# Seven block products for eight in three pairs of row tiles, inside the attention slots of an attention and mixer kernel

## The chip, the cores and the metric

One core of one Trainium2 chip. The metric is the device time of one execution in microseconds (us). The kernel is a single program of about ten thousand instructions on five engines: TensorE (PE) for matrix products, VectorE (DVE), ScalarE (ACT) and GpSimd (POOL) for elementwise work, SyncE (SP) as the queue that issues most transfers.

## The reference

Cosine attention over 8 batches of 12 heads, 448 rows, head width 64; then a mixer of a token layer and a channel layer.

```
q_n = q / (norm(q) + 1e-6);  k_n = k / (norm(k) + 1e-6)
attn = softmax(q_n @ k_n^T / tau)            # tau = 0.1
x = (attn @ v) as (8, 448, 768)
h = relu(x^T @ w_tok1) @ w_tok2              # 448 -> 256 -> 448, over the rows
u = x + h^T
out = u + relu(u @ w_ch1) @ w_ch2            # 768 -> 1536 -> 768, over the channels
```

Inputs and output are float32; the kernel multiplies in float16 and accumulates in float32.

## The kernel before

**Slots.** The work runs over 48 pairs of heads, `i` = 0 to 47, six to a batch. What is done for one `i` of the main loop is called a slot here. A slot begins with the scores of pair `i` (`score`, three tiles of 128 keys for both heads, Exp on ACT, which also leaves the softmax unnormalised), goes on with attention times values of pair `i - 1` (`pv_rest`, `pv`; DVE takes the reciprocal and scales: `x`), and then has, in the order in which PE meets them: a unit of channel work, the rest score (`score_rest`, the last 64 keys), the second token product of pair `i - 2` (`tok2`, into `u16`, transposed by a transfer on SP's queue into `ut`: `udma`), more channel units, and the first token product of pair `i - 1` (`tok1`).

**Preparing q and k.** Beside it a slot prepares later pairs. `square` and `sums` form the squared lengths of pair `i + 3` (squares on POOL or ACT, the sum on DVE), `norms` makes 1/norm for pair `i + 2` (Ln and Exp on ACT, a sum and a reciprocal on DVE), `scaled` multiplies k and q by it on POOL into a float16 tile `kq`, and `tpose_dma` transposes that by a transfer on SP's queue into `qk`, which the scores of slot `i + 2` read. SP also issues the loads of q, k and v for pairs `i + 6` and `i + 4` and the stores of the output. Every engine takes its own instructions in order.

**Buffers.** q and k tiles have 7 buffers each, v 4, `kq` 4, `qk` 4, tiles of squares 3. PSUM has two pools: `ps2` with three double banks (scores, and channel units that are called `wide`), `ps` with two single banks.

**The channel layers.** Batches 0 to 5 go through them inside the slots; the rows of a batch form three tiles of 128 and a shared tile `m = 3` that holds the last 64 rows of two batches. `m_ch1` makes one of 12 blocks of the hidden layer (six matmuls of 448 columns, Relu on ACT into `gt`). `m_ch2` makes one half (384 columns) of one row tile: 12 matmuls, then DVE adds `u` and SP stores the finished rows. Before, a queue of units with a rate for each stretch of slots (`refill`, `due`, `RATES`) decides which unit goes into which slot.

**The end.** Batches 6 and 7, and three row tiles of batch 5, go through a block form of the channel layers after the last slot. There a product of 2 x 2 blocks is made from seven block products instead of eight (`p1` to `p7`, `q1` to `q7`). It needs sums of the weight blocks: `fast_weights2` forms four sums of quarters of the second weight matrix on POOL, each in three parts; before, five parts stand in slots 40 to 44 and seven after the last slot.

Of the kernel before, what the change touches and what calls it, by code (L numbers as in the profile page):

```python
# [22 lines left out]
def kernel(  # L23
# [12 lines left out]
    nc = tc.nc  # L36
# [44 lines left out]

    cst = ctx.enter_context(tc.tile_pool(name="cst", bufs=1))
# [4 lines left out]
    att = late.enter_context(tc.tile_pool(name="att", bufs=4))  # L87
    qkv = ctx.enter_context(tc.tile_pool(name="qkv", bufs=7, side="right"))
# [14 lines left out]
    def load_first(a, src):  # L103
        t = qkv.tile([SC, QS, E], FP32, name=f"{a}f_0", tag=f"{a}f", bufs=7)
        for g, eng in ((0, nc.sync), (1, nc.scalar)):
            eng.dma_start(out=t[:, NCH * g:NCH * (g + 1)].rearrange("p c e -> p (c e)"),
                          in_=src[0, g].rearrange("(p c) e -> p (c e)", c=NCH))
        return t

    def pool_of(nm):  # L110
        return att if nm == "v" else qkv

    def load_rows(i, nm, src, bufs):
        h0 = 2 * (i % NPAIR)
        if old(i):
            t = pool_of(nm).tile([SC, QS, E], FP32, name=f"{nm}f_{i}", tag=f"{nm}f", bufs=bufs)
            nc.sync.dma_start(
                out=t[:].rearrange("p (g c) e -> p g (c e)", g=2),
                in_=src[h0:h0 + 2].rearrange("g (p c) e -> p g (c e)", c=NCH))
            return t  # L120
        t = pool_of(nm).tile([128, 2 * KC, E], FP32, name=f"{nm}f_{i}", tag=f"{nm}f", bufs=bufs)
        nc.sync.dma_start(out=t[:].rearrange("p (g c) e -> p g (c e)", g=2),
                          in_=src[h0:h0 + 2, 0:128 * KC].rearrange("g (p c) e -> p g (c e)", c=KC))
        return t

    def load_rest(i, nm, src):
        h0 = 2 * (i % NPAIR)
        t = (att if nm == "v" else rest).tile([128, HP, E], FP32, name=f"{nm}r_{i}", tag=f"{nm}r", bufs=4)
        for g in range(2):
            nc.sync.dma_start(out=t[64 * g:64 * g + 64],  # L130
                              in_=src[h0 + g:h0 + 2 * HP:2, 128 * KC:S].rearrange("j p e -> p j e"))
        return t

    def load_qk(i):
        b, h0 = i // NPAIR, 2 * (i % NPAIR)
        n = i // HP
        half.setdefault(n, {})
        st = pipe[i] = {}
        st["q"] = qkv.tile([SC, QS, E], FP32, name=f"qf_{i}", tag="qf")
        nc.sync.dma_start(out=st["q"][:].rearrange("p (g c) e -> p g (c e)", g=2),  # L140
                          in_=q[b, h0:h0 + 2].rearrange("g (p c) e -> p g (c e)", c=NCH))
        st["k"] = load_rows(i, "k", k[b], 7)
        if not old(i) and "kr" not in half[n]:
            half[n]["kr"] = load_rest(i, "k", k[b])

    def load_v(i):
        pipe[i]["v"] = load_rows(i, "v", v[i // NPAIR], 4)
        if not old(i) and "vr" not in half[i // HP]:
            half[i // HP]["vr"] = load_rest(i, "v", v[i // NPAIR])
# [15 lines left out]
    NV = 3  # L165
# [46 lines left out]
    kqs = [rest.tile([128, 2, NCH, 2, E], FP16, name=f"kq{i}", bufs=1) for i in range(4)]  # L212
    sqs = [rest.tile([128, 2 * QS, E], FP32, name=f"sq{i}", bufs=1) for i in range(3)]
# [23 lines left out]
    def square(i, a, act=False):  # L237
        st = pipe[i]
        sl, np_ = lay(i)
        if "sq" not in st:  # L240
            st["sq"] = sqs[i % 3]
        parts = [(st["kq"[a]][:], st["sq"][0:np_[a], sl[a]])]
        if a == 0 and not old(i):
            parts = [(st["k"][:], st["sq"][:, 0:2 * KC]),
                     (half[i // HP]["kr"][:, i % HP], st["sq"][:, 2 * KC])]
        for src, dst in parts:
            if act:
                nc.scalar.activation(out=dst, in_=src, func=AF.Square)  # L248
            else:
                nc.gpsimd.tensor_mul(out=dst, in0=src, in1=src)  # L250
# [33 lines left out]
    def scale_part(i, a, c0, c1, eng):  # L284
        st = pipe[i]
        if "kq16" not in st:
            st["kq16"] = kqs[i % 4]
# [5 lines left out]
    def scale(i, a, eng=None):  # L293
# [3 lines left out]
        if "kq16" not in st:  # L297
            st["kq16"] = kqs[i % 4]
# [165 lines left out]
    def m_ch1(b, ct, wide):  # L464
        if b // 2 not in gts:
            gts[b // 2] = mix.tile([128, CT, 2 * S], FP16, name=f"gt_{b // 2}", tag="gt", bufs=1)
        gt = gts[b // 2]
# [7 lines left out]

    ost = {}


    def m_ch2(b, m, lo, hi, st, wide):
        gt = gts[b // 2]  # L480
# [36 lines left out]
    def ch1_units(b):  # L517
        return [(ns(S, DT), lambda wide, ct=ct: m_ch1(b, ct, wide), False, b % 2 == 0) for ct in range(CT)]

    def ch2_units(b):  # L520
        cuts = ((0, DH, None), (DH, D, 0))
        if b == 0:
            order = [(m, c) for c in cuts for m in range(3)]
        else:
            order = [(m, c) for m in range(3) for c in cuts]
            if b == KEPT_B:
                order = [(3, c) for c in cuts]
            elif b % 2:
                order[3:3] = [(3, cuts[0])]
                order[5:5] = [(3, cuts[1])]  # L530
        return [(ns(hi - lo, CT), lambda wide, m=m, lo=lo, hi=hi, st=st: m_ch2(b, m, lo, hi, st, wide), m == 3, False)
                for m, (lo, hi, st) in order]

    HD, HC = DT // 2, CT // 2
# [67 lines left out]
    def gpart(i, b, d):  # L602
        lo = 64 * b
        return (gts["new"] if b else gts[KEPT_B // 2])[:, HC * i + 2 * d:HC * i + 2 * d + 2, lo:lo + S]

    def g_shared(i):
        nc.sync.dma_start(out=gts["new"][:, HC * i:HC * (i + 1), 0:64],
                          in_=gts[KEPT_B // 2][:, HC * i:HC * (i + 1), 384:S])
# [39 lines left out]
    def fast_weights2(n, parts=range(3)):  # L648
        def w(i, j):
            return [wc2t[:, HC * i + 2 * m:HC * i + 2 * m + 2, DH * j:DH * (j + 1)] for m in range(3)]  # L650

        t = fw.setdefault("t2", {})
        if n not in t:
            at = [(n - 1 + m) % 2 for m in range(3)]
            t[n] = [qkv.tile([128, 2, DH], FP16, name=f"t{n}w2_{m}", tag=("qf", "kf")[z]) for m, z in enumerate(at)]
        a, b = {1: (w(0, 1), w(0, 0)), 2: (w(1, 1), t.get(1)), 3: (w(1, 1), w(0, 1)), 4: (w(1, 0), t.get(2))}[n]
        for m in parts:
            tt(nc.gpsimd, t[n][m][:], a[m], b[m] if n % 2 else b[m][:], ALU.subtract)

    def fast_w2(n, j):  # L660
# [3 lines left out]
        return fw["t2"][{4: 4, 5: 1, 6: 2, 7: 3}[n]][j // 2][:, j % 2]  # L664
# [4 lines left out]
    def gtile(t, i):  # L669
        g, at = (gts["new"], t - 3) if 3 <= t < 7 else (gts[KEPT_B // 2], t if t < 3 else t - 3)  # L670
        return g[:, HC * i:HC * (i + 1), 128 * at:128 * at + 128]

    def s_tile(g, k):
        if g == 0 and k < 3:
            return qkv.tile([128, HC, 128], FP16, name=f"s{k}g_0", tag=("qf", "kf")[k - 1])[:]
# [112 lines left out]
    queue = []  # L788
    fed = [0.0, 0.0]

    def unit(wide=False, late=False):
        if queue:
            swap = late and queue[0][2] and len(queue) > 1 and not queue[1][2] and not queue[1][3]
            t, fn = queue.pop(1 if swap else 0)[:2]
            fn(wide)
            fed[0] -= t

    def due():
        return queue and fed[0] > queue[0][0] / 2

    KEPT = 6000.0
    RATES = {2 * NPAIR + 2: 4550.0, 4 * NPAIR + 2: 4100.0, 5 * NPAIR + 2: 3850.0, 6 * NPAIR + 2: 3200.0}
    LATE = NP_ALL - 10
    ACT_SQ = range(LATE - 2, NP_ALL - 3)

    def refill(b):
        new = ch1_units(b) + ch2_units(b)
        if b == 0:
            fed[1] = (sum(u[0] for u in new) - KEPT) / (NPAIR + 1)
        if b == KEPT_B:  # L810
            queue[:0] = new[:CT]
            queue[-4:-4], new = new[CT:], []
        queue.extend(new)

    with tc.manual_schedule():
# [127 lines left out]
        def side(i):  # L943
# [6 lines left out]
            elif i + 3 < NP_ALL:  # L950
                squares(i + 3)
            if i in (8, 11):
# [13 lines left out]
        for i in range(NPAIR + 1, NP_ALL):  # L966
# [18 lines left out]
            if i == NPAIR + 1:  # L985
                refill(0)
            elif pj == (3 if b - 1 == KEPT_B else 2) and 1 < b < B - 1:
                refill(b - 1)
# [4 lines left out]
            fed[1] = RATES.get(i, fed[1])  # L993
            if i == NP_ALL - HP:
                fed[1] = (sum(u[0] for u in queue) - fed[0]) / HP
            fed[0] += fed[1]
            unit(True)
# [4 lines left out]
            if i in ACT_SQ:  # L1002
                square(i + 3, 1, act=True)
            if i > NPAIR + 1:
# [3 lines left out]
            if due():  # L1008
                unit(True, True)
            while due():  # L1010
                unit()
            tok1(i - 1)
            if i + 3 < NP_ALL:
                sums(i + 3)
            if NP_ALL - 8 <= i < NP_ALL - 5:
                fast_weights2(1, (i - NP_ALL + 8,))
            if NP_ALL - 5 <= i < NP_ALL - 3:
                fast_weights2(2, (i - NP_ALL + 5,))
# [10 lines left out]
        while queue:  # L1029
            unit(True)  # L1030
# [31 lines left out]
        fast_weights2(2, (2,))  # L1062
        fast_weights2(3)
# [9 lines left out]
        fast_weights2(4)  # L1073
# [101 lines left out]
```

## Time and profile before

| | |
|---|---|
| median of 3 runs | 381.85 us (379.79 to 382.25) |
| profiled execution, its own time | 379.98 us |
| span from first to last instruction | 378.2 us |
| PE busy | 365.3 us, 4090 matmuls |
| DVE busy | 253.7 us |
| ACT busy | 239.1 us |
| POOL busy | 286.6 us |
| transfers | 64.65 MB, mean 171 GB/s |
| granted TensorE clock | 1.000 |

The span is the stretch that the profile sees; the time of an execution holds 1.8 us more around it. Busy times of different engines overlap. A busy PE is not PE at its peak, because the recorded ends of matmuls overlap with the next ones; the distance from one start to the next is the better measure of what a matmul costs.

In the profile a line reads: where (line and engine), operation, what is written and read, shape, number, then busy time and the mean of one in nanoseconds, then the idle time ahead of it on its engine and what ended that. A line of a timeline begins with its start in us from the span's start and its length.

### The profile page before, as it was taken

The page shows a single profiled execution, that of the slowest core. Times are in us where ns is not written, and L with a number is a line of the kernel's source. Part 1 is how long each engine was busy: PE and PEld are TensorE (multiplying, and loading weights), DVE is VectorE, ACT ScalarE, POOL GpSimd, SP SyncE. Part 2 cuts the span into 40 slices and gives each one's busy share as a digit, 9 for nine tenths or more (in the row PEclk, how much of TensorE's full clock was granted, in tenths as well). Part 3 has the DMA queues.
Part 4 walks back from the last instruction along what each step waited for, and adds up shares of the span by engine and source line. Part 5 has one row for each costly group of instructions (what it writes and reads, how often), then busy time and mean ns, then how long its engine had stood idle before and what let it go on. Part 6 is the DMA issues. An engine that isn't in the chain of part 4 may idle for free.

```text
span 378.2 us, 10337 instructions
## 1 busy us (share of the span) xinstructions
PE 365.3 (97%) x4090; PEld 239.5 (63%) x4090; DVE 253.7 (67%) x568; ACT 239.1 (63%) x413; POOL 286.6 (76%) x413
## 2 busy tenths in 40 slices
PE   7789999999999999999999999999999999999994
PEld 6566666676566666667666666566666665555663
DVE  7888866776446765546636577465657778797872
ACT  6999887855675547744768447787887634255110
POOL 8899998979675685668677687747799843897753
PEclk9999999999999999999999999999999999999999
DMA  7999999999987899767798988988697572103244
GB/s 210 264 250 191 266 252 217 215 171 176 224 201 163 170 213 215 178 142 169 194 210 166 193 159 214 233 172 180 145 208 111 124 130 55 23 1 92 86 128 125
DMA packets 118225, 64.65 MB, mean 171 GB/s; under 512 B 74272, under 2 KB 114848, under 8 KB 118176
## 3 DMA queue, kind: packets, MB, share of 16 engines
q1 hardware_dynamic: 111984, 58.25, 70.4%
q0 software_dynamic: 5616, 5.21, 9.8%
q8 instruction: 32, 0.52, 0.6%
q10 hardware_dynamic: 576, 0.52, 0.5%
q14 instruction: 17, 0.14, 0.2%
HBM read 43.45 MB, written 11.01 MB: 144 GB/s over the span
## 4 chain that ended last, share of the span: by engine, by line
PE 82%; DVE 7%; ACT 4%; POOL 3%; DMA 2%; issue 1%; ACTq 0%; DVEq 0%; POOLq 0%
PE psG L471 20%; PE psF L487 18%; PE psO L388 9%; PE psS L349 7%; PE psU L438 5%; PE psR L424 4%; PE psYo L699 4%; ACT pt L350 3%; PE psY L594 3%; PE psZo L699 3%; PE psXo L699 3%; DVE ssq L266 2%; PE psQ L356 2%; PE psZ L594 2%; PE psO L371 1%; DMA qk<-kq 1%
## 5 line engine op out<-in xcount | busy, mean ns | idle before, releaser
L350 ACT ACTIVATE pt<-psS 128x896 f16<-128x896 f32 (+1 forms) x156 | 135.8, 911 | 46.0 <-PE psS L349 46.0
L471 PE MATMUL psG<-ut,wc1t 128*128 128x448 f16 x432 | 89.3, 352 | 0.0
L302 POOL TENSOR_TENSOR kq<-kf,rn 128x384 f16<-128x384 f32 (+1 forms) x47 | 41.8, 890 | 56.0 <-DVE rn L279 55.9
L487 PE MATMUL psF<-wc2t,gt 128*128 128x384 f16 x432 | 75.7, 326 | 0.0
L471 PEld LDWEIGHTS <-wc1t 128*128 128x128 f16 x432 | 40.2, 97 | 32.1
L266 DVE TENSOR_REDUCE ssq<-sq 128x15 f32<-128x960 f32 (+2 forms) x51 | 56.1, 1100 | 2.7 <-ACT sq L248 1.8
L474 ACT ACTIVATE gt<-psG 128x448 f16<-128x448 f32 x72 | 39.0, 542 | 28.9 <-PE psG L471 28.9
L487 PEld LDWEIGHTS <-gt 128*128 128x128 f16 x432 | 40.5, 98 | 24.0
L427 DVE TENSOR_SCALAR rt<-psR 128x256 f16<-128x256 f32 x48 | 20.1, 418 | 48.0 <-PE psR L424 48.0
L302 POOL TENSOR_TENSOR kq<-qf,rn 112x512 f16<-112x512 f32 x45 | 47.0, 1045 | 3.0
L491 DVE TENSOR_TENSOR ost<-psF,u 128x384 f32<-128x384 f32 (+1 forms) x42 | 23.4, 557 | 34.4 <-PE psF L487 34.3
L349 PE MATMUL psS<-qk 64*128 64x448 f16 x312 | 41.0, 353 | 3.3 <-DVE qk L328 2.5
L441 DVE TENSOR_TENSOR u<-psU,x 128x512 f16<-128x512 f32 x48 | 33.1, 690 | 13.0 <-PE psU L438 12.0
L250 POOL TENSOR_TENSOR sq<-kf 128x384 f32<-128x384 f32 (+1 forms) x46 | 40.2, 873 | 0.7 <-DMA kf<-in_k_dram 0.4
L388 PE MATMUL psO<-vt,pt 128*128 128x65 f16 (+1 forms) x1024 | 39.2, 193 | 0.0
L392 DVE TENSOR_TENSOR x<-psO,rec 128x256 f16<-128x256 f32 x82 | 34.8, 425 | 2.8
L388 PEld LDWEIGHTS <-pt 128*128 128x128 f16 (+1 forms) x1024 | 34.2, 97 | 3.5 <-issue 0.9
L250 POOL TENSOR_TENSOR sq<-qf 112x512 f32<-112x512 f32 x30 | 31.2, 1040 | 0.0
L424 PEld LDWEIGHTS <-w1t 128*128 128x128 f16 x384 | 24.9, 98 | 8.3 <-issue 2.1
L438 PEld LDWEIGHTS <-w2t 128*128 128x128 f16 x384 | 24.8, 98 | 8.4 <-POOL w2t L198 0.9
L438 PE MATMUL psU<-rt,w2t 128*128 128x128 f16 x384 | 29.3, 219 | 0.8 <-POOL w2t L198 0.8
L424 PE MATMUL psR<-x,w1t 128*128 128x128 f16 x384 | 29.3, 219 | 0.2 <-DVE u L441 0.2
(139 smaller groups left out, 524.4 us busy)
## 6 DMA issues: line engine op xcount, KB each, us to landing
qf<-in_q_dram SPq DMA_DIRECT2D x47, 224.0 KB, 4.1
kf<-in_k_dram SPq DMA_DIRECT2D x36, 192.0 KB, 3.8
vf<-in_v_dram SPq DMA_DIRECT2D x36, 192.0 KB, 3.8
vf<-in_v_dram SPq DMA_DIRECT2D x12, 224.0 KB, 8.5
kf<-in_k_dram SPq DMA_DIRECT2D x11, 224.0 KB, 8.7
wc1t<-in_moe_w_ch_dram POOLq DMA_DIRECT2D x4, 576.0 KB, 10.6
wc2t<-in_moe_w_ch_dram POOLq DMA_DIRECT2D x2, 1152.0 KB, 14.1
out_dram<-ost SPq DMA_DIRECT2D x5, 336.0 KB, 3.7
```

Of the source, the lines that this page charges most:

```text
L250: nc.gpsimd.tensor_mul(out=dst, in0=src, in1=src)
L266: nc.vector.tensor_reduce(out=st["ssq"][0:n, sl], in_=st["sq"][0:n, sl], axis=AXX.X, op=ALU.add)
L302: eng.tensor_tensor(out=kq[0:p, a, 0:n].rearrange("p c g e -> p g c e"), in0=st["kq"[a]][:].rearrange("p (g c) e -> p g c e", g=2), in1=_b ...
L349: nc.tensor.matmul(psS[:, hh, 0:S], qk[hb, c * n:c * n + 128], qm[hb], start=True, stop=True)
L350: nc.scalar.activation(out=pts[i % 2][0:n, 2 * S * c:2 * S * (c + 1)].rearrange("p (h s) -> p h s", h=2), in_=psS[0:n, :, 0:S], func=AF.Ex ...
L388: nc.tensor.matmul(psO[:, m, 0:E + 1], pts[i % 2][0:n, at:at + 128], vt[0:n, i % HP, nch * hh + c, 0:E + 1], start=(old(i) and c == 0), st ...
L424: nc.tensor.matmul(psR[:, tt], w1t[:, w1[m], tt * 128:(tt + 1) * 128], st["x"][:, m], start=(m == 0), stop=(m == 3))
L438: nc.tensor.matmul(psU[:, m], w2t[:, tt, lo:lo + 128], st["rt"][:, tt], start=(tt == 0), stop=(tt == TT - 1))
L471: nc.tensor.matmul(psG[:, 0:S], wc1t[:, dt, ct * 128:(ct + 1) * 128], ut[b][:, dt].rearrange("p m s -> p (m s)")[:, lo:lo + S], start=(dt ...
L474: nc.scalar.activation(out=gt[:, ct, (b % 2) * S:(b % 2 + 1) * S], in_=psG[:, 0:S], func=AF.Relu)
L487: nc.tensor.matmul(psF[:, 0:hi - lo], gt[:, ct, at:at + 128], wc2t[:, ct, lo:hi], start=(ct == 0), stop=(ct == CT - 1))
L699: nc.tensor.matmul(out[:, o:o + hi - lo], a[:, j], fast_w2(n, j)[:, lo:hi], start=(start and j == 0), stop=(j == HC - 1), skip_group_check ...
```

## The change

Three pairs of row tiles, `G1` = tiles 1 and 2 of batch 2, `G2` = tiles 0 and 1 of batch 3, `G3` = tiles 0 and 1 of batch 4, get the second channel layer in block form inside the slots, seven products of six matmuls per pair instead of four half products of twelve.

- `sg_first` (slots 28, 34, 41) makes products 1, 2, 6 and 7 of a pair, into the two halves of one double bank `psY`, and DVE adds each result into the rows of the output; `sg_second` (slots 29, 35, 42) makes products 5, 4 and 3 into `psZ`.
- The four sums of row tiles that a pair needs (`sg_sum`) are made on POOL in four slots each (26 to 29, 32 to 35, 39 to 42).
- The twelve parts of the sums of weights go to slots 14 to 25, all on POOL, into a tile `tw` of their own.
- Room for it: q and k have rings of 5 buffers, with `tw` lent as further buffers for pairs 5, 6, 12 and 13 and as third tile of squares until slot 14; `qk` 3 for 4, `kq` 3 for 4, squares 2 for 3 later on, value tiles 2 for 3.
- The squares of q of slots 14 to 35 go from POOL to ACT (`ACT_SQ`), as those of slots 36 to 44 did.
- The queue of units is replaced by a list written out by hand, `WORK`. At the end, slots 44 to 47 hold a ch1 block with a half product, and then one half product each; before, they held two, one, two and one.

```diff
+    def sg_sum(n, r1, r2):
+        s1, s2, s3 = [t[:] for t in sgs]
+        out, a, b, op = {1: (s1, part(*r2, 0), part(*r2, 1), ALU.add),
+                         2: (s2, s1, part(*r1, 0), ALU.subtract),
+                         3: (s3, part(*r1, 0), part(*r2, 0), ALU.subtract),
+                         4: (s2, part(*r1, 1), s2, ALU.subtract)}[n]
+        tt(nc.gpsimd, out, a, b, op)
+
+    def sg_prod(n, r1, r2, out, start=True):
+        s1, s2, s3 = sgs
+        a = {1: lambda: part(*r1, 0), 2: lambda: part(*r1, 1), 3: lambda: s2, 4: lambda: part(*r2, 1),
+             5: lambda: s1, 6: lambda: s2, 7: lambda: s3}[n]()
+        for j in range(HC):
+            nc.tensor.matmul(out[:, 0:DH], a[:, j], fast_w2(n, j), start=(start and j == 0), stop=(j == HC - 1),
+                             skip_group_check=True)
+
+    def sg_add(out, src, other):
+        tt(nc.vector, j3(out), j3(src[:, 0:DH]), j3(other) if len(other.shape) == 2 else other, ALU.add)
...
+    def sg_first(r1, r2):
+        def head():
+            st = slot_g[r1] = {}
+            st["o"] = [outp.tile([128, D], FP32, name=f"osg_{r[0]}_{r[1]}", tag="ost") for r in (r1, r2)]
+            y = st["y"] = ps2.tile([128, 2, 512], FP32, name=f"psY_{r1[0]}_{r1[1]}", tag="s")
+            o1 = st["o"][0]
+            sg_prod(1, r1, r2, y[:, 0])
+            sg_add(o1[:, 0:DH], y[:, 0], u_of(r1, 0))
+            sg_prod(2, r1, r2, y[:, 1])
+            sg_add(o1[:, 0:DH], y[:, 1], o1[:, 0:DH])
+
+        def middle():
+            st = slot_g[r1]
+            sg_prod(6, r1, r2, st["y"][:, 0], False)
+            sg_add(st["o"][0][:, DH:D], st["y"][:, 0], u_of(r1, 1))
+
+        def end():
+            st = slot_g[r1]
+            sg_prod(7, r1, r2, st["y"][:, 0], False)
+            for h in (1, 0):
+                sg_add(st["o"][1][:, DH * h:DH * (h + 1)], st["y"][:, 0], u_of(r2, h))
...
+    def sg_second(r1, r2):
+        def head():
+            st = slot_g[r1]
+            z = st["z"] = ps2.tile([128, 2, 512], FP32, name=f"psZ_{r1[0]}_{r1[1]}", tag="s")
+            o2 = st["o"][1]
+            sg_prod(5, r1, r2, z[:, 0])
+            sg_add(o2[:, DH:D], z[:, 0], o2[:, DH:D])
+            sg_prod(4, r1, r2, z[:, 1])
+            sg_add(o2[:, 0:DH], z[:, 1], o2[:, 0:DH])
+            sg_store(r2, o2)
+
+        def end():
+            st = slot_g[r1]
+            o1 = st["o"][0]
+            sg_prod(3, r1, r2, st["z"][:, 0], False)
+            sg_add(o1[:, DH:D], st["z"][:, 0], o1[:, DH:D])
+            sg_store(r1, o1)
...
+    G1, G2, G3 = ((2, 1), (2, 2)), ((3, 0), (3, 1)), ((4, 0), (4, 1))
+    WORK = {
...
+        25: run(2, 8, 12), 26: halves(2, 0), 27: run(3, 0, 3), 28: run(3, 3, 4), 29: run(3, 4, 5),
+        30: run(3, 5, 9), 31: run(3, 9, 12), 32: halves(3, 3), 33: halves(3, 2),
+        34: run(4, 0, 1), 35: run(4, 1, 2), 36: run(4, 2, 5), 37: run(4, 5, 9), 38: run(4, 9, 12),
+        39: run(5, 0, 3), 40: run(5, 3, 6), 41: run(5, 6, 7), 42: run(5, 7, 8), 43: run(5, 8, 11),
+        44: run(5, 11, 12) + [ch2(4, 2, 0)], 45: [ch2(4, 2, 1)], 46: [ch2(5, 3, 0)], 47: [ch2(5, 3, 1)],
+    }
+    FIRST = {28: G1, 34: G2, 41: G3}
+    SECOND = {29: G1, 35: G2, 42: G3}
+    SUMS = {i: (lambda n=n, m=m: fast_weights2(n, m))
+            for i, (n, m) in enumerate([(n, m) for n in (1, 2, 3, 4) for m in range(3)], 14)}
...
-    ACT_SQ = range(LATE - 2, NP_ALL - 3)
+    ACT_SQ = range(14, NP_ALL - 3)
...
+            todo = WORK[i]
+            first = sg_first(*FIRST[i]) if i in FIRST else None
+            second = sg_second(*SECOND[i]) if i in SECOND else None
+            if first or second:
+                (first or second)[0]()
+            else:
+                todo.pop(0)(True)
             if old(i):
                 score(i, KC)
             else:
                 score_rest(i)
             if i in ACT_SQ:
                 square(i + 3, 1, act=True)
+            if first:
+                first[1]()
             if i > NPAIR + 1:
                 tok2(i - 2)
             if i + 1 < DMA_T0:
                 tpose(i + 1)
-            if due():
-                unit(True, True)
-            while due():
-                unit()
-            tok1(i - 1)
+            if first:
+                tok1(i - 1)
+                first[2]()
+            elif todo and not second:
+                todo.pop(0)(True)
+            for fn in todo:
+                fn(False)
+            if second:
+                second[1]()
+            if not first:
+                tok1(i - 1)
```

## The prediction

> **What bounds the kernel now.** I read the page first, then TensorE's waits, then the timeline of one attention slot.
>
> ```profile
> span 378.2 us, 10337 instructions
> PE 365.3 (97%) x4090; PEld 239.5 (63%) x4090; DVE 253.7 (67%) x568; ACT 239.1 (63%) x413; POOL 286.6 (76%) x413
> L487 PE MATMUL psF<-wc2t,gt 128*128 128x384 f16 x432 | 75.7, 326 | 0.0
> L491 DVE TENSOR_TENSOR ost<-psF,u 128x384 f32<-128x384 f32 (+1 forms) x42 | 23.4, 557 | 34.4 <-PE psF L487 34.3
> ```
>
> PE is busy 97% of the span. A mean of 326 ns per matmul contains overlap: the twelve of a half product take 1.95 us in the chain of waits (1.95 / 12 = 0.1625 us each). Six of 448 columns take 1.14 us. So PE streams almost without gaps, and its list of waits is short. From 80 to 360 us it is this (us in all, times, longest):
>
> ```profile
> PE psS L349 <- DMA qk<-kq: 0.2, 1, 0.2
> PE psO L371 <- DVE u L441: 0.2, 1, 0.2
> ```
>
> Whatever PE no longer has to do is saved; whatever it waits for is lost. The slot that starts at 220.11 gives the clockwork of a slot with channel-2 products:
>
> ```profile
> 221.69 2.11 PE L487 MATMUL psF<-wc2t,gt 128*128 128x384 f16 x12
> 222.13 0.31 ACT L281 ACTIVATE rn<-ssq,tiny 128x15 f32<-128x15 f32 x1
> 222.47 0.22 ACT L282 ACTIVATE ne<-rn 128x15 f32<-128x15 f32 x1
> 222.74 0.18 DVE L275 TENSOR_REDUCE rn<-ne 128x15 f32<-128x30 f32 x1
> 222.95 0.25 DVE L279 RECIPROCAL rn<-rn 128x15 f32<-128x15 f32 x1
> 223.63 0.35 PE L356 MATMUL psQ<-qk 128*128 128x448 f16 x1
> 223.84 1.14 DVE L491 TENSOR_TENSOR ost<-psF,u 64x384 f32<-64x384 f32 x2 [0.64 <-PE psF L487]
> ```
>
> The products start 1.58 us after the slot; DVE first has to finish the norms, at 223.20 (3.09 us into the slot). The add of psF starts 0.04 us after the product's modelled end (221.69 + 2.11 = 223.80).
>
> **What is removed.** Each pair of row tiles had 4 half products of 12 matmuls = 48; now it has 7 products of 6 = 42. Three pairs: 18 matmuls fewer, 18 x 0.1625 = **-2.9 us** on PE.
>
> **What is added on PE's path: three waits per pair.** In the built program's list of instructions with their waits, the first matmul of product 2 (it writes psY[:, 1]) waits for DVE at the count of the add that reads product 1 out of psY[:, 0]; product 6 waits for the add of product 2; product 4 for the add of product 5. The two halves of the tile are thus guarded as one. Products 7 and 3 also wait, but behind other work. PE takes its matmuls in order, so behind product 2 stand the rest score, product 6, tok2 and all else of the slot. I lay the new sequence over the slot above.
>
> (a) Product 1 is six matmuls from 221.69 on, 0.975 us; product 2 could start at 222.67. DVE is free at 223.20, its add takes 0.557: 223.76. From a DVE end to a PE start I take 0.06, from a row at 300 us (u ends at 299.90 + 0.69 = 300.59, the waiting matmul starts at 300.65). Product 2 starts at 223.82: PE stands for **1.15 us**.
>
> (b) Product 2 has issued all at 224.79 and ends at 224.95 (a group's modelled end is 2.11 - 1.95 = 0.16 after its last issue). Add from 224.99 to 225.55, product 6 at 225.61. Between them PE has only the rest score (0.19, start to start 223.63 to 223.82), to 224.98: **0.63 us**.
>
> (c) In the second slot product 5 and 4 do what 1 and 2 did: 1.15. But here the slot before ends with a ch1 group directly ahead of the scores, whose Relu (0.55) keeps ACT to 0.74 us into the slot, where the first Exp starts at 0.41 in the slot shown. Norms and add come 0.33 later: **1.48 us**.
>
> Per pair 3.26, for three **+9.8 us**. Floor: with an idle DVE a wait is still 0.16 + 0.04 + 0.56 + 0.06 = 0.82; (b) then stays 0.63, so 2.27 per pair and 6.8 in all. Ceiling: DVE another reciprocal and x (0.6) late in (a) and (c): 4.5 per pair, 13.4 in all. I take 9.8, since its rows are of the very slot shape. PE's clock should not fall: from 8.5 to 39.2 us PE is busy 26.00 of 30.70 us, with the granted clock at 1.00.
>
> One page bears on this. The Trainium skill, "PSUM — Partial Sum Buffer", summary of rules, advises reading one bank while the matmul runs into a different one, and guarding by bank. The head does put products 1 and 2 into two banks, so by that rule (a), (b) and (c) would all vanish and the sum be about -2.7 us; the program's waits guard the tile, and no row of before has a product and a read on two halves of one tile. The sum goes by the waits.
>
> **What lies beside other work.** 22 squares of q go from POOL (1.04 us) to ACT (0.63), slots 14 to 35. Cover: ACT waits 46.0 us in all for psS; the slots from 258.64 to 277.35 already have this square and three Relu, and take 6.24 us like those without it. Uncovered it would be 22 x 0.63 = 13.9. 24 sums go onto POOL, 12 of weights and 12 of row tiles, at the 1.64 us of the t1w rows. Seven of the weight sums came after 323 us before, where PE doesn't wait for POOL; five in slots 40 to 44. Cover: POOL waits for rn 34 times, 55.9 us, 1.64 each, right where a sum goes, and the square leaves 1.04 there. Without it the scaling of k and q is late, then its transpose on SP's queue, then the scores two slots on; at 239.11 a score is reached with 0.22 us of such a wait.
>
> 12 adds more on DVE (24 for 12, 6.7 us) are the waits above or idle time. Rings of 5 (q, k) for 7: a load in slot i takes the buffer scaled in slot i-1, so nothing waits; if POOL were a slot late, the load would be, and with it everything on SP. The stores keep their number; the second one of a pair waits for an add at the end of its slot, with the next ut and qk transposes queued behind it, but scaling ends 5.8 us into a slot, so the queue is free by then. psY and psZ hold one of three double buffers until their last adds: 0.2 + 1.11 us after product 7, against ch1 and one score (1.14 + 0.37). So 0, with 0 to +1 for the range.
>
> Elsewhere: the wait for qk at 239 us goes with the longer slots, -0.3. At the end slots 46 and 47 get one half product each where slot 46 had two; score 47 comes 2.4 us sooner, against a transpose that lands some 9.3 us after slot 45's start (issue at 5.85, median 3.4), needed at 9.4, and the m = 3 adds (1.14) hold up psO as at 300.65. +0.5, between -0.3 and +1.8.
>
> **Sum.** -2.9 + 9.8 - 0.3 + 0.5 = **+7.1 us**: span 378.2 to 385.3, the profiled execution 379.98 to 387.1. The median of the runs is 381.85, which would make 388.9; between the two I put **388.0**. With the floor it is +3.9 to +4.1 (384 to 386), with the ceiling +11.
>
> **Rivals.** *The waits are hidden, and the removed matmuls count.* Place: the nine waits in slots 28, 29, 34, 35, 41, 42. For it: two banks, and a DVE that is idle for a third of the span. Time: -2.9 - 0.3 + 0.5 = -2.7, 377.3 to 379.2. It decides once the nine cost under 2.9 us together, 0.32 each. Against it: the add alone is 0.557 and only the rest score (0.19) stands between one product and the next, and only for (b).
>
> *The freed time is taken back in another place on top.* POOL, with 1.64 more in slots of 6.24, falls behind by some 0.5 a slot in the five shortest slots with a sum, or SP's queue does in the slots with five stores: +2 to +3 on the scores, 389.1 to 391.9. Against it: the 1.64 us that POOL waits each time.
>
> *The change doesn't do what it says.* If the seven products were issued as eight, PE would keep its 4090 matmuls; the built list has 4072, so this is out.
>
> *The floor holds.* DVE's norms come sooner than in the row, and the sum is +4: 384 to 386. It is the low part of my case.
>
> **How the numbers follow.** My case, PE stopped by the adds, +3.9 to +9.5: 0.81. Hidden waits: 0.09. Lateness on top: 0.07. Something else that makes it faster by over 1%: 0.03. About 1% is what a measurement of this kernel can tell from no change. Slower by over 1% (over 3.8 us) is the first and third, less a little at the floor: 0.85. Within 1%: the second and that edge, 0.12. Faster: 0.03. The range, 383.5 to 391.0, holds the case from its floor up, and the start of the lateness.
>
> **What the profile after would show.** PE 4072 matmuls. In TensorE's waits, psY and psZ behind a DVE add of the output tile, 9 times, 0.6 to 1.5 us each, 7 to 10 in all. The first-product slots last some 9.6 us (2.83 + 4 x 0.975 + 1.14 + 1.78) and the second ones 8.4. No wait of PE for POOL in slots 14 to 45. I am wrong if psY is not in that list, if a score waits for its transpose in slot after slot, or if POOL's wait for rn is gone.

## The result, and the profile after

Median 386.88 us (386.73 to 387.29, 4 runs) against 381.15 us of the kernel before (379.79 to 382.25, 4 runs): ratio 1.0154, 95% interval 1.0115 to 1.0192. The change makes the kernel 1.5% slower. (One execution of a variant below, 387.35 us at a granted clock of 0.988, is a slow one and stands in its range but not in its ratio.) The profiled execution took 386.73 us, with a span of 385.0 us against 378.2: 6.8 us longer, at a granted clock of 1.00 in both.

The page after, its first lines:

```profile
span 385.0 us, 10389 instructions
PE 364.1 (95%) x4072; PEld 237.2 (62%) x4072; DVE 256.8 (67%) x579; ACT 251.5 (65%) x435; POOL 282.8 (73%) x402
```

PE has 18 matmuls fewer and is busy 95% of the span, not 97%. Its list of waits (us in all, times, longest), from 84 to 303 us, where the slots with channel-2 work lie, has new lines at the top:

```profile
PE psY L684 <- DVE osg L542: 3.9, 6, 0.9
PE psZ L684 <- DVE osg L542: 2.6, 3, 0.9
PE psS L361 <- DVE ost L502: 0.6, 2, 0.3
```

The first two are the nine waits of products for adds. The third was not foreseen. The timeline of slot 28, which starts at 179.56, shows waits (a) and (b) of the prediction (start, length, engine, line, operation; in brackets the idle time ahead of it and what ended it):

```profile
181.11 1.14 PE L684 MATMUL psY<-wc2t,gt 128*128 128x384 f16 x6
182.38 0.25 DVE L291 RECIPROCAL rn<-rn 128x15 f32<-128x15 f32 x1
182.55 0.50 DVE L542 TENSOR_TENSOR osg<-psY,u 128x384 f32<-128x384 f32 x1
183.10 1.14 PE L684 MATMUL psY<-wc2t,gt 128*128 128x384 f16 x6 [0.85 <-DVE osg L542]
184.08 0.35 PE L368 MATMUL psQ<-qk 128*128 128x448 f16 x1
184.28 0.56 DVE L542 TENSOR_TENSOR osg<-psY,osg 128x384 f32<-128x384 f32 x1 [1.23 <-PE psY L684]
184.89 1.14 PE L684 MATMUL psY<-tw,sg 128*128 128x384 f16 x6 [0.46 <-DVE osg L542]
```

Product 1 starts at 181.11 and has issued its six matmuls 0.975 us later, at 182.085. Product 2 starts at 183.10: PE lost 1.02 us. The bracket says 0.85, because it counts from product 1's modelled end (181.11 + 1.14 = 182.25). Between product 2 and product 6 PE has one matmul (psQ, 0.19 from start to start): 184.08 + 0.19 = 184.27, and product 6 starts at 184.89, 0.62 later, where the bracket says 0.46. A bracket or a list of waits gives the lower side of what PE loses; the distance from start to start gives all of it. The second slot of the pair starts at 188.96:

```profile
189.50 1.72 ACT L362 ACTIVATE pt<-psS 128x896 f16<-128x896 f32 x2
190.63 1.14 PE L684 MATMUL psZ<-tw,sg 128*128 128x384 f16 x6
191.91 0.25 DVE L291 RECIPROCAL rn<-rn 128x15 f32<-128x15 f32 x1
192.08 0.49 DVE L542 TENSOR_TENSOR osg<-psZ,osg 128x384 f32<-128x384 f32 x1
192.63 1.14 PE L684 MATMUL psZ<-tw,gt 128*128 128x384 f16 x6 [0.87 <-DVE osg L542]
```

Wait (c): 192.63 - (190.63 + 0.975) = 1.03 us. So a pair loses 1.02 + 0.62 + 1.03 = 2.67 us, and three pairs 8.0.

The unforeseen line is that of the shared tiles `m = 3`. In the hand-written order their two halves fill slots 19 and 32, and the second of them sits in a double bank when slots 20 and 33 begin:

```profile
121.66 2.11 PE L498 MATMUL psF<-wc2t,gt 128*128 128x384 f16 x12
123.81 1.14 DVE L502 TENSOR_TENSOR ost<-psF,u 64x384 f32<-64x384 f32 x2 [0.74 <-PE psF L498]
125.02 0.36 PE L361 MATMUL psS<-qk 64*128 64x448 f16 x2 [0.31 <-DVE ost L502]
```

This tile needs two adds of 64 rows (rows of two batches), 1.14 us together, and the third score of slot 20 (`psS`, 125.02) takes the bank that they read. Slots 20 and 33 take 7.35 and 7.36 us, where the same slot takes 6.65 without it: 1.4 us in all.

What the span gained and lost, from the lengths of the slots: matmuls -2.9, nine waits +8.0, `m = 3` tiles +1.4, the wait for qk in slot 35 gone -0.4, slots 44 to the end +0.2 (2.6 us shorter, where 2.8 us of units moved to earlier slots), the first 40 us +0.7. That makes +7.0; the span shows +6.8, so about 0.2 is left over, and no term under that size can be told apart here.

### The profile page after: what moved, and what is told of

Read it like the earlier page. It is cut to its first block, busy times and chain, and to the rows that moved or that the text cites. A ratio compares the mean times of both kernels' runs of the same rounds, so it can differ in the third digit from the quotient of the medians.

```text
span 385.0 us, 10389 instructions
## 1 busy us (share of the span) xinstructions
PE 364.1 (95%) x4072; PEld 237.2 (62%) x4072; DVE 256.8 (67%) x579; ACT 251.5 (65%) x435; POOL 282.8 (73%) x402
## 4 chain that ended last, share of the span: by engine, by line
PE 79%; DVE 8%; ACT 4%; DMA 4%; issue 1%; POOL 1%; SPq 0%; DVEq 0%; POOLq 0%
PE psG L481 21%; PE psF L498 12%; PE psO L400 8%; PE psS L361 6%; PE psU L450 5%; PE psR L436 4%; DMA kf<-in_k_dram 4%; PE psYo L778 4%; ACT pt L362 3%; PE psY L596 3%; PE psY L684 3%; PE psZo L778 3%; PE psXo L778 3%; DVE ssq L278 2%; PE psZ L596 2%; PE psZ L684 2%
## 5 line engine op out<-in xcount | busy, mean ns | idle before, releaser
L314 POOL TENSOR_TENSOR kq<-kf,rn 128x384 f16<-128x384 f32 (+1 forms) x43 | 38.0, 885 | 54.4 <-DVE rn L291 53.6
L278 DVE TENSOR_REDUCE ssq<-sq 128x15 f32<-128x960 f32 (+2 forms) x45 | 50.0, 1111 | 2.8 <-ACT sq L260 2.7
L498 PE MATMUL psF<-wc2t,gt 128*128 128x384 f16 x288 | 50.7, 326 | 0.0
L314 POOL TENSOR_TENSOR kq<-qf,rn 112x512 f16<-112x512 f32 x41 | 42.8, 1044 | 2.8
L498 PEld LDWEIGHTS <-gt 128*128 128x128 f16 x288 | 26.8, 98 | 15.6
L262 POOL TENSOR_TENSOR sq<-kf 128x384 f32<-128x384 f32 (+1 forms) x38 | 32.5, 854 | 0.6 <-DMA kf<-in_k_dram 0.6
L369 ACT ACTIVATE pt<-psQ 128x448 f16<-128x448 f32 x36 | 19.6, 544 | 19.7 <-PE psQ L368 19.7
L502 DVE TENSOR_TENSOR ost<-psF,u 128x384 f32<-128x384 f32 (+1 forms) x30 | 16.7, 556 | 19.1 <-PE psF L498 17.0
```

Of the source, the lines that this page charges most:

```text
L278: nc.vector.tensor_reduce(out=st["ssq"][0:n, sl], in_=st["sq"][0:n, sl], axis=AXX.X, op=ALU.add)
L314: eng.tensor_tensor(out=kq[0:p, a, 0:n].rearrange("p c g e -> p g c e"), in0=st["kq"[a]][:].rearrange("p (g c) e -> p g c e", g=2), in1=_b ...
L498: nc.tensor.matmul(psF[:, 0:hi - lo], gt[:, ct, at:at + 128], wc2t[:, ct, lo:hi], start=(ct == 0), stop=(ct == CT - 1))
```

## The experiments

The kernel before was timed again beside each set of variants: 380.06 us beside split tiles, plain, shared tiles first and both; 380.21 beside no sums, squares on POOL, order in place of tiles and the two edits; 379.96 beside order in the second slots alone and the store edit alone. Ratios are to these.

**Split tiles.** Is it the guard on the tile, or the adds as such? Products 2 and 4 go into single banks of their own from the other pool, with the order on PE unchanged:

```diff
-            y = st["y"] = ps2.tile([128, 2, 512], FP32, name=f"psY_{r1[0]}_{r1[1]}", tag="s")
+            y = st["y"] = ps2.tile([128, 512], FP32, name=f"psY_{r1[0]}_{r1[1]}", tag="s")
+            y2 = ps.tile([128, 512], FP32, name=f"psV_{r1[0]}_{r1[1]}", tag="b")
...
-            sg_prod(2, r1, r2, y[:, 1])
+            sg_prod(2, r1, r2, y2)
...
-            sg_prod(4, r1, r2, z[:, 1])
+            sg_prod(4, r1, r2, z2)
```

> The changed kernel, with the two halves of psY and of psZ as two tiles: products 1, 6, 7 (5, 3) in a double bank of ps2 as before, product 2 (4) in a single bank of ps. Theory W (the loss is PE standing behind DVE's adds, because both halves count as one tile): the three waits per pair go, 1.0 + 0.6 + 1.0 us in the trace after, 8.0 us over three pairs; span 385.0 to 377.0, time some 378.8. The list of TensorE's waits has no psY and no psZ of over 0.1 us. Rival B (the loss comes with the smaller rings, the squares on ACT and the sums on POOL): none of these is touched, time 386 to 387. Rival C (the waits only move): product 6 or the scores of the next slot wait instead, 382 to 386.

Measured: 379.08 us (378.64 to 382.97), ratio 0.9975 (0.9949 to 1.0001), span 377.4. The first slots fall from 9.40 to 7.76 us, which is (a) + (b) = 1.64. The timeline of slot 28:

```profile
180.98 1.14 PE L684 MATMUL psY<-wc2t,gt 128*128 128x384 f16 x6
181.96 1.14 PE L684 MATMUL psV<-wc2t,gt 128*128 128x384 f16 x6
182.42 0.50 DVE L542 TENSOR_TENSOR osg<-psY,u 128x384 f32<-128x384 f32 x1
```

Product 2 follows product 1 after 0.98 us, 0.46 before the add of product 1 has even begun. The adds are the same number at the same length; only what waits for them is gone. The second slots fall from 7.93 to 7.08, 0.85 for the 1.03 of (c): the first-layer unit after product 4 (`psG`; the second token layer ahead of it is done at 191.45) now starts 0.17 late, 0.05 us after the add that frees the bank of product 4:

```profile
191.01 0.56 DVE L542 TENSOR_TENSOR osg<-psW,osg 128x384 f32<-128x384 f32 x1 [0.20 <-PE psW L684]
191.62 1.30 PE L481 MATMUL psG<-ut,wc1t 128*128 128x448 f16 x6
```

The separate allocation alone turns the change from 1.5% slower into no loss.

**Plain.** What does the rest of the change cost? The three pairs get ordinary half products back, with rings, squares, sums and list as in the change:

```diff
-        25: run(2, 8, 12), 26: halves(2, 0), 27: run(3, 0, 3), 28: run(3, 3, 4), 29: run(3, 4, 5),
+        25: run(2, 8, 12), 26: halves(2, 0), 27: run(3, 0, 3), 28: halves(2, 1) + run(3, 3, 4), 29: halves(2, 2) + run(3, 4, 5),
...
-    FIRST = {28: G1, 34: G2, 41: G3}
-    SECOND = {29: G1, 35: G2, 42: G3}
+    FIRST = {}
+    SECOND = {}
```

> The changed kernel without its block form: the three pairs get 4 half products of 12 matmuls each as before (PE 4090 matmuls), in the same slots; the sums on POOL for the pairs are still made, but nothing reads them; smaller rings, squares on ACT, weight sums in slots 14 to 25 and the list of work stay. Theory W: the waits (8.0) go and the 18 matmuls (2.9) come back: 386.9 - 8.0 + 2.9 = 381.8, some 1 us over the kernel before, of which 1.4 are the m = 3 slots. Rival B: these other parts are the loss, so 386 or more (the 2.9 us on top: 389).

Measured: 381.34 us (380.83 to 387.35), ratio 1.0022 (1.0004 to 1.0040), span 379.5. So everything but the products costs 1.3 us by the two spans, and slots 20 and 33 alone have 1.4 of it (7.35 and 7.36, with the same wait for `ost`). The profiles of plain and of split also have a score at 84 us that waits for `qk` (0.49 and 0.43 in the brackets); the profiles of the change and of most other variants lack it, and no run shows why. So sums, squares, rings and the list cost nothing that can be told from such differences, some 0.5 us. From plain to split is what seven products for eight are worth once nothing waits: 2.1 us of the 2.9. The rest lies in the second slots, 0.28 in each: the unit's late start (0.17), and 0.11 at the head of the slot, where the two groups of attention products start 0.33 apart in split and 0.22 in plain.

**Shared tiles first.** In the slots of the `m = 3` tiles each half is made first, with a half of another tile behind it:

```diff
-        19: halves(1, 3), 20: halves(1, 0),
+        19: [ch2(1, 3, 0), ch2(1, 0, 0)], 20: [ch2(1, 3, 1), ch2(1, 0, 1)],
...
-        30: run(3, 5, 9), 31: run(3, 9, 12), 32: halves(3, 3), 33: halves(3, 2),
+        30: run(3, 5, 9), 31: run(3, 9, 12), 32: [ch2(3, 3, 0), ch2(3, 2, 0)], 33: [ch2(3, 3, 1), ch2(3, 2, 1)],
```

> The changed kernel, with only the order in slots 19, 20, 32 and 33 altered: the half products of the shared tile m = 3 come first in their slots, and the second place goes to a half product of a full tile. In the trace after, slots 20 and 33 hold 0.87 and 0.88 us of PE standing still where slots of that kind hold 0.19: a score there waits for the double bank that the two 64-row adds (1.14 us) of the m = 3 product just before it still read. Theory W: 2 x 0.69 = 1.4 us less, some 385.4. Rival (the standing still comes from the transposes or from ACT): no change, 386.9, and slots 20 and 33 keep 7.35 us.

Measured: 385.88 us (384.84 to 387.77, 4 runs), ratio 1.0139 (1.0091 to 1.0188). Slots 20 and 33 take 6.65 each, so the 1.4 us came back there, as expected; slot 27 took 0.2 more. The span of the profiled run, 386.0, hides it, because that run reached slot 7 at 42.02 us, where the change reached it at 39.85. The medians differ by 1.0 with intervals that overlap, so the mechanism is shown by the slots and not by the time.

**Both.** The two edits together.

> Both edits together: two tiles for the halves, and the m = 3 products first in slots 19, 20, 32, 33. Theory W: 8.0 + 1.4 = 9.4 us less than the changed kernel, span 375.6, time some 377.4, about 1% under the kernel before. If the two gains overlap or come back as another wait: 379 to 382. Rival B: 385 to 387.

Measured: 378.74 us (378.42 to 379.21), ratio 0.9956 (0.9939 to 0.9973), span 376.9. Faster than before, but less than the sum of the two edits. Slot 35 took 7.80 where split had 7.08. The timeline there:

```profile
224.28 1.66 SPq L523 DMA_DIRECT2D out_dram<-ost  x2
...
227.75 0.84 SPq L517 DMA_DIRECT2D out_dram<-ost  x2
228.57 0.56 DVE L542 TENSOR_TENSOR osg<-psY,u 128x384 f32<-128x384 f32 x1 [1.55 <-PE psG L481]
229.65 0.36 PE L361 MATMUL psS<-qk 64*128 64x448 f16 x2 [0.66 <-DVE osg L542]
```

The bracket of the add at 228.57 names PE, which had been done with product 7 for 1.2 us (product 7 starts at 226.22 and ends at 226.22 + 1.14 = 227.36), so it must be another. The chain of waits of the same stretch names it (start, length, what):

```profile
224.94 0.36 SPq L523
...
225.41 3.03 DMA out_dram<-ost
...
228.57 0.10 DVE osg L542
```

The output buffer that product 7's adds write is the one of the `m = 3` tile of block 3 (in the built program the add waits for that tile's stores). Its last add now ends one slot later, at 218.86 in place of 215.31 in split, and SP, with two transposes and the loads of q, k and v ahead in its queue, issued the stores from 224.28 on. The store edit below tests this.

**No sums.** Are the 24 sums on POOL really covered? On top of both, this kernel leaves the sums out and the products read weights and rows directly, so its output is not the answer and only its time counts:

```diff
-        return tw[:, {4: 3, 5: 0, 6: 1, 7: 2}[n], j]
+        return wc2t[:, HC * (n % 2) + j, 0:DH]
...
-        a = {1: lambda: part(*r1, 0), 2: lambda: part(*r1, 1), 3: lambda: s2, 4: lambda: part(*r2, 1),
-             5: lambda: s1, 6: lambda: s2, 7: lambda: s3}[n]()
+        a = {1: lambda: part(*r1, 0), 2: lambda: part(*r1, 1), 3: lambda: part(*r1, 1), 4: lambda: part(*r2, 1),
+             5: lambda: part(*r1, 0), 6: lambda: part(*r1, 1), 7: lambda: part(*r2, 0)}[n]()
...
-            if i in SUMS:
-                SUMS[i]()
```

> The version with split tiles and the m = 3 halves first, without the 24 sums on POOL (12 of weights, 12 of rows; 1.64 us each, 39.4 in all): the products read the weights and rows themselves, with the same shapes and counts on PE, so their results are left wrong in this run and only its time is read. Theory (POOL's sums lie in time in which POOL waited for the norms): no change, 378.7 (378.2 to 379.2), and POOL's wait for rn grows by most of the 39. Rival (each sum pushes the scaling of the queries and keys back, and PE meets it in the transposed tiles): faster by 1 us or more, 377.7 or less, with fewer waits of PE for qk or DVE work in slots 14 to 42.

Measured: 378.80 us (377.84 to 381.26), ratio 0.9961 (0.9937 to 0.9985), the time of both to 0.1 us. POOL's waits, first both, then this run:

```profile
POOL kq L314 <- DVE rn L291: 46.6, 35, 3.2
```

```profile
POOL kq L314 <- DVE rn L291: 86.4, 39, 4.3
```

39.8 us of idle time came in place of 39.4 us of sums, and the time did not move by more than its interval; slot 35 still takes 7.71.

**Squares on POOL.** How much cover is left? `ACT_SQ` as before the change, on top of both:

```diff
-    ACT_SQ = range(14, NP_ALL - 3)
+    ACT_SQ = range(LATE - 2, NP_ALL - 3)
```

> The same version with the query squares of slots 14 to 35 back on POOL (22 of 112 x 512, 1.04 us each there; 0.62 on ACT), where the kernel before had them. Theory (the covers are real but finite): POOL is busy 73.7 of the 81.6 us of slots 14 to 25 in the split version with m = 3 first; with 12.5 more it needs 86.2, 4.6 more than there is; slots 26 to 35 have 70.9 for 55.4 + 10.4 = 65.8 and take theirs. So 378.7 + 4.6 = 383.3 (381.5 to 386, since POOL also has waits that it cannot fill). Rival (POOL's wait for rn has room for both): 378.7, same. Rival (POOL falls behind in every one of the 22 slots): 22 x 1.04 = 22.9, over 400.

Measured: 380.63 us (380.21 to 383.35), ratio 1.0010 (0.9990 to 1.0030): 2 us slower than both, less than half of the 4.6 expected. In its profile 22 squares (22.9 us) cost 2.2 us in three slots: 17 (7.15 for 6.24), 22 (7.27 for 6.95) and 35 (8.81 for 7.80). In PE's waits from 84 to 303 us:

```profile
PE psS L361 <- DVE osg L542: 1.7, 1, 1.7
PE psS L361 <- DMA qk<-kq: 1.1, 2, 0.8
```

The second line is POOL's lateness: scaling late, transpose late, a score waits. The first is the same output buffer as in both, whose stores SP issued 4.88 us into slot 34 in place of 3.63, behind its transposes and loads. My sum of busy time against slot length took POOL's work to be bound to the slots that it is seen in. POOL's wait for rn was still 28.7 us here, down from 46.6 in both, so part of the squares went into gaps that the sum had not counted. So moving the squares off POOL is worth 2 us once the sums are there.

**Order in place of tiles.** The change with whole tiles, and work put between the products:

```diff
             if first or second:
                 (first or second)[0]()
...
-            if first:
-                first[1]()
+            if first or second:
+                todo.pop(0)(False)
+                (first or second)[1]()
             if i > NPAIR + 1:
                 tok2(i - 2)
+            if first:
+                first[2]()
```

> The changed kernel with its two-bank tiles psY and psZ kept whole; only PE's order inside the six slots differs. In a first-product slot product 1 is followed by the last score piece and one first-layer unit (0.19 + 6 x 0.19 = 1.33 us of matmuls), then product 2, the second token layer (8 matmuls, 0.45), product 6, the first token layer (0.45), product 7. In a second-product slot product 5 is followed by the score piece and the first-layer unit (1.33), then product 4, the second token layer (0.45), product 3. Theory (a product waits for the vector add that still reads its tile, and pays only what nothing covers): from the trace of the change product 2 can start 1.02 after product 1's end, product 6 0.81 after product 2's, product 4 1.03 after product 5's. Covers of 1.33, 0.45 and 1.33 leave 0, 0.36 and 0; new are product 7 behind product 6's add (0.2 left, as the token layer's own vector work stands ahead of it) and product 3 behind product 4's add (0.36 left): 0.9 for a pair in place of 2.67, 2.7 for three in place of 8.0. Span 385.0 - 5.3 = 379.7, time 381.5 (380.5 to 383). Rival (the cost is fixed to two products in one tile, or to reading and writing one tile at all, and no order helps): 386.9 as before. Rival (what is pushed back, the exponentials of the last score piece and the token layers, ends later in its place): between the two, 383.5 or more, with the new idle time on PE in front of the next slot's scores or token layers.

Measured: 385.92 us (383.92 to 386.42, 4 runs), ratio 1.0124 (1.0090 to 1.0158), span 384.1: a miss by 4.4 us. Part of it is the start of the profiled run (slot 7 at 41.65 us, 1.8 later than the change). The first slots fell from 9.40 to 8.49, where 8.3 was expected, but the second slots stayed at 7.96. The timeline at the seam:

```profile
188.79 1.14 PE L684 MATMUL psY<-tw,sg 128*128 128x384 f16 x6 [0.20 <-DVE osg L542]
189.97 1.02 DVE L542 TENSOR_TENSOR osg<-psY,u 128x384 f32<-128x384 f32 x2 [0.90 <-PE psY L684]
191.04 0.36 PE L361 MATMUL psS<-qk 64*128 64x448 f16 x2 [0.63 <-DVE osg L542]
```

With the first-layer unit moved forward, product 7 is the last work of its slot. Its two adds (1.02) still read the double bank when the third score of the next slot takes it. The unit had been the cover of product 7's adds; I had spent it twice.

**Order in the second slots alone.** The same reordering only where nothing large stands behind the last product.

```diff
+            if second:
+                todo.pop(0)(False)
+                second[1]()
             if i > NPAIR + 1:
                 tok2(i - 2)
...
             if second:
-                second[1]()
+                second[2]()
```

> The changed kernel with its two-bank tiles whole and its first-product slots as they are; in the second-product slots alone product 5 is followed by the last score piece and the first-layer unit (1.33 us of matmuls), then product 4, the second token layer, product 3. Theory (in the version with both kinds of slot reordered the first slots gave back what they won, because product 7 came last in its slot and the next slot's third score took the bank that its two adds, 1.02 us, still read): with product 7 in its old place the second slots keep their gain, 1.03 for product 4 less 0.20 for product 3 behind product 4's add, so 7.93 - 0.83 = 7.10 each, span 385.0 - 2.5 = 382.5, time 384.3 (383.5 to 385). Rival (the second slots of that version stayed at 7.96 because the unit or product 3 costs as much in its new place): 386.9, no gain.

Measured: 385.06 us (385.01 to 385.10, 4 runs), ratio 1.0125 (1.0104 to 1.0146), span 383.2. The second slots take 7.26, 7.27 and 7.27: 0.66 less each, 2.0 in all, against 0.83 and 2.5 expected. The rival is out, and the time misses my bound of 385 by 0.06. The rest is product 3 behind product 4's add:

```profile
194.08 0.61 PE L450 MATMUL psU<-rt,w2t 128*128 128x128 f16 x8
194.90 1.14 PE L684 MATMUL psZ<-wc2t,sg 128*128 128x384 f16 x6 [0.20 <-DVE osg L542]
```

Eight matmuls of the token layer take 0.45 from start to start, so product 3 could have begun at 194.53 and lost 0.37. I had put in the 0.20 of the bracket in the other reordered kernel: the error described above, made by me after I had read it.

**Two edits toward a best version.** On top of both, the stores of that `m = 3` tile are issued by ACT, and in the second slots the first token layer comes ahead of the unit:

```diff
-                nc.sync.dma_start(out=out[bb].rearrange("(p c) d -> c p d", c=NCH)[c, p0:p1], in_=o[r:r + 64])
+                (nc.scalar if b == 3 else nc.sync).dma_start(
+                    out=out[bb].rearrange("(p c) d -> c p d", c=NCH)[c, p0:p1], in_=o[r:r + 64])
...
-            elif todo and not second:
+            elif second:
+                tok1(i - 1)
+            elif todo:
...
-            if not first:
+            if not first and not second:
                 tok1(i - 1)
```

> The version with split tiles and the m = 3 halves first, with two further edits. (1) The two stores of the m = 3 tile of block 3 are issued by ACT, not SP: in that version they were issued on SP at 224.28, 5.4 us after their last add (218.86), behind four loads, and the second product slot of the second pair lost 0.66 us because the adds of product 7 take that output buffer and the next score takes the bank that they read. Without it slot 35 takes 7.08 again in place of 7.80: -0.7. (2) In the second-product slots the first token layer comes ahead of the first-layer unit, which waited about 0.2 us for the add that reads psW: -0.2 each, -0.5 in all. Span 376.9 - 1.2 = 375.7, time 377.5 (376.9 to 378.2). Rival: the waiting stores hold up ACT's exponentials, or the token layer meets the same bank instead of the unit; then 378.7 or more.

Measured: 379.75 us (379.34 to 381.96), ratio 0.9979 (0.9962 to 0.9997): slower than both. The store edit worked, since slot 35 no longer differs from 29 and 42. The token layer lost: these slots take 7.40, 0.32 more than in split, and the slots after them 0.24 more. PE's waits from 84 to 303 us:

```profile
PE psS L361 <- DVE osg L543: 0.5, 3, 0.2
PE psG L481 <- DVE u L453: 0.5, 3, 0.2
```

The unit now waits for the bank of the second token layer (0.69 us of DVE work), and product 3, moved to the end of its slot, holds the double bank that a score of the next slot takes: the seam of the reordered kernel again.

**The store edit alone.** On top of both.

> The version with split tiles and the m = 3 halves first, with one edit: the two stores of the m = 3 tile of block 3 are issued by ACT in place of SP. Theory (the adds of product 7 of the second pair wait for the buffer of that tile to be stored): slot 35 takes 7.08 in place of 7.80 and nothing else moves, span 376.9 - 0.7 = 376.2, and with the start of the run at the middle of the profiles so far 375.7; time 377.5 to 378.2. Rival (ACT holds its exponentials behind the two stores, which wait for the adds): slot 33 or 34 longer by as much, 378.7.

Measured: 377.86 us (377.67 to 378.22), ratio 0.9936 (0.9918 to 0.9955), span 376.0: the fastest of all, 2.1% under the change by the two ratios. Slot 35 takes 7.08. The issue stands on ACT where the adds end, 6 us earlier than on SP:

```profile
218.12 1.37 ACTq L523 DMA_DIRECT2D out_dram<-ost  x2
219.53 0.54 ACT L369 ACTIVATE pt<-psQ 128x448 f16<-128x448 f32 x1 [2.35 <-DVE u L453]
220.87 1.73 ACT L362 ACTIVATE pt<-psS 128x896 f16<-128x896 f32 x2 [0.27 <-PE psS L361]
```

The waits for the buffer are gone, so the cause given for slot 35 in both is shown. The rival was half there: the two stores hold up the exponential of the rest score (2.35 us of idle time ahead of it, 0.53 in both). It has slack, and the next exponentials start 0.40 us after their scores, as in both; PE lost 0.06 by it (slot 34 took 7.85 for 7.79). From 84 to 303 us no wait of PE is left that the list would name. Not all of the span's gain reached the time: an execution holds some 2.1 us around the span here and in the kernel with two edits (378.1 against 376.0), in both 1.8. Only these two kernels issue those stores from ACT; where the 0.3 us comes from is open.

## Why the prediction was right, point by point

**The waits.** Nine of them, behind the named adds, as read from the program. (a) 1.02 for 1.15, (b) 0.62 for 0.63, (c) 1.03 for 1.48; 8.0 us for 9.8. First slots of 9.40 for 9.6, second of 7.93 for 8.4. The term that was mis-sized is (c): I made the norms 0.33 late behind the Relu of the slot before. The Exp behind that Relu started 0.54 into the slot (189.50), not 0.74 as I had put it, and the reciprocal of rn ended 3.20 into the slot (192.16) against 3.09 in the row that I used: 0.1 late, not 0.33. Both adds behind the norms also came earlier than I had them. They began inside the recorded length of the reciprocal ahead (182.55 for an end at 182.63) and took 0.50 and 0.49, where I had 0.557 from the reciprocal's end: 0.14 of (a) and of (c). The last 0.09 of (c) is product 5 itself, which started 1.67 into the slot for my 1.58.

**The rule that spoke against the sum.** The two banks of one tile did not help; with a tile for each bank the waits were gone, 7.4 us of them. The Trainium skill, "PSUM — Partial Sum Buffer", summary of rules, advises to read one bank while the matmul runs into another and to guard by bank. Split tiles agree with it: product 2 ran through the whole 0.50 us of the add on product 1's bank and cost nothing. The change had two banks, but its program guards them as one tile, and the waits followed the guard.

**What was left out.** The 1.4 us of the `m = 3` tiles. I had that row in front of me (64 rows, two adds, 1.14) and used it only for the last slots. The step that failed is that I followed the products that the diff adds and not the half products whose slots `WORK` reassigns. By luck it offset most of the 1.8 us by which the waits were put too high: 9.8 forecast against 8.0 + 1.4.

**What lies beside other work.** Right as far as the runs can tell: sums 0 (no sums), the rest of the change together 1.3, where `m = 3` alone has 1.4 (plain). The double banks' hold, put at 0 with 0 to +1, was 0, but by a margin that one moved unit used up (order).

**Small terms.** qk at 239 us: -0.4 for -0.3. End: +0.2 for +0.5.

**The total.** Span +6.8 for +7.1, the profiled execution 386.73 for 387.1. My 388.0 lay above the median because I leaned on a median of before of 381.85 from three runs; later sets gave 380.0 to 380.2. That the span came within 0.3 is partly luck: besides the offset above, 0.7 of the 6.8 lies in the first 40 us and is no part of the forecast (last section).

**The rivals.** Hidden waits were one allocation away: split tiles took 379.08, and their condition (under 2.9 us for the nine) is met there. Lateness of POOL or SP on top did not occur in the change; it shows, at 2 us, where the squares are put back on POOL.

## What to carry to other kernels

In this program a wait belongs to the tile that is allocated, so two results that are read one after the other go into two tiles, even where one tile already spans two banks; here that was worth 7.4 us, more than the 6.8 that the whole change lost. Work that covers one wait may already cover another, in the next slot through the ring of buffers: before a unit is moved, list what its present neighbour hides behind it. A reordered store is part of the ring of its buffer too: ask who writes that buffer next, and in which queue the store stands.

## What was not expected of the hardware

An add of 64 rows by 384 takes as long as one of 128 rows: 1.14 us for two against 0.56 for one. Covering a tile in two halves of rows so doubled DVE's time here, and the hold on its bank.

The first 40 us vary from one profiled execution to the next by more than most effects looked for here. Over the eleven profiles of the changed kernel and its variants, slot 7 began between 39.17 us (squares on POOL) and 42.02 us (shared tiles first), with no edit ahead of it. The kernel before had 39.18. So this evidence can't put the +0.7 of the account above down to the change, and single spans were compared here by the lengths of their slots.
